# The drain of an attention pipeline from PSUM, and the last expert matmuls in column halves

## The chip, the cores and the metric

The kernel runs on one core of a Trainium2 chip. Its metric is device time in microseconds (us), the median of several runs. A core has TensorE (PE, with its weight loads, PEld), VectorE (DVE), ScalarE (ACT), GpSimd (POOL) and SyncE (SP), which issues the DMAs here. Each runs its own queue in order; semaphores tie them together.

## The reference, cut to what matters

```python
# attention, 4 batches x 8 heads, 576 rows of 64, each row keeps its 32 largest scores
scores = q @ k.T / 8;  kth = 32nd largest of each row
x = softmax(where(scores >= kth, scores, -1e9)) @ v      # as 2304 tokens x 512
# soft mixture of experts, 8 experts with 4 slots each
logits = x @ phi                                          # 2304 x 32
d = exp(logits - logits.max(0));  d /= d.sum(0) + 1e-9
slot_in = (d.T @ x)                                       # 32 x 512
slot_out[e] = relu(slot_in[e] @ w1[e]) @ w2[e]            # w1 512x1024, w2 1024x512
x = softmax(logits, over slots) @ slot_out
# feed-forward, 512 -> 2048 -> 512 with a piecewise quadratic
h = x @ w_in;  g = where(h >= 1, h, where(h <= -1, 0, (h + 1)**2 / 4));  out = g @ w_out
```

## The kernel before, in words

**Attention.** There are 16 pairs (a batch and two heads), each of five row blocks. The step of a block is a token: a letter, the block, for most the head, and behind the point the pair. `S` score matmuls, `C` their copy out of PSUM, `G` and `L` the search for the largest, `M`, `V`, `Y`, `K` the rest of that search (`M` and `Y` on DVE, `V` and `K` on POOL), `P`, `U`, `E` the masked exponential (for the last two blocks of the last pair `U` is a DVE operation, line 853), `T` the transposes, `Q` and `R` their copies, `A` the matmuls with v, `H` the scaled result. A list in the code, `TAIL`, gives the order of the last pairs by hand: each engine takes its own tokens from it in this order.

**The drain.** For the last batch the logits come in three pieces of columns (0 to 256, 256 to 512, 512 to 576; `last_mix`), with tokens `n` + letter + piece: `a`, `b` the logits into PSUM bank n (line 757), `c` their copy to `lT` (760), `d` the running maximum (764, 765), `e` the exponential (773), `f` the factor for the older sum, `t` transposes (782), `g` their copies (791, 794), `w` the weighing of x into `pu` (721), `x` the update of `acc` (798), `l` and `y` bookkeeping on DVE. Block 4 is the middle piece, piece 2. `jp`, `jd` join sums. `fl`, `xc` turn and copy the last x into `xT`. `sp` transposes `acc` (737), `sa` copies it to `siT` (739), which the experts read. All three banks are one tile, `lm_ps`; the transposes `T` of the last pair share one tile of two halves, `lt_ps`, taken in turn.

**The experts.** Two groups of four. `ex_in` multiplies `siT` by w1 (line 1049), `ex_relu`, `ex_turn`, then `ex_out` by w2 (1072) over eight chunks c, four experts side by side in the four column groups; chunks c and c+1 share one loaded tile per expert. `ex_save` copies the result, `ex_place` turns it (1084) and places it in `so128` (1088). `m_first` multiplies by w_in (1129), a copy and a difference follow (1132, 1136), and the first `emit_h` (1207) opens the last stage: 96 steps of one `emit_h` and nine matmuls (1255). `tell`, with a transpose and a maximum, forms a flag that tells if a slower second body must run; `mix_load` to `mix_turn` prepare the combine weights in between.

**The loads.** 88 weight tiles of 512 KB are loaded by SP in one fixed order (`worder`): w1, w2 (with two tiles of w_out in between, as numbers 39 and 40), then w_in and w_out. Each goes to a slot of memory that comes free, and a load waits for its slot's last reader; all behind it on SP wait too. While attention runs there are few slots; `TAIL` frees some with certain tokens (`frees`), as `T31`, `T21`, the last `Y`, `U`, `A`. After attention seven slots `wB0` to `wB6` are laid over the memory of the attention's pools, in the order in which these were opened (`p_work` first, then `p_small`, `p_xT`, `p_xh`, `p_moe`): numbers 39 to 45 of the loads go there, the two w_out tiles first. The next reuse the slots of w1 as `ex_in` ends with them, first those of its chunk 0.

Of the kernel before, what the change touches and what calls it, by code (L numbers as in the profile page):

```python
# [77 lines left out]
Y01.14 m09.11 C30.14 z4.14 O11.14 K10.14 T30.13 Q30.13 S31.14 U31.13 B0.14 L2.14 X10.14 K11.14
E31.13 m10.11 X11.14 C31.14 P00.14 G30.14 Y10.14 U40.13 T31.13 G31.14 M20.14 P01.14 Q31.13 M21.14
Y11.14 A20.13 L3.14 S40.14 R3.13 A21.13 O20.14 U00.14 K20.14 E40.13 C40.14 B1.14 O21.14 T40.13  # L80
Q40.13 X20.14 c0.15 c1.15 S00.15 E00.14 M30.14 K21.14 P10.14 T41.13 G40.14 H2.13 R4.13 U01.14 X21.14
V30.14 c4.15 Y20.14 K30.14 Q41.13 A30.13 P11.14 C00.15 T00.14 E01.14 S01.15 U10.14 Q00.14 M31.14
A31.13 C01.15 E10.14 U11.14 H3.13 Y21.14 T01.14 B2.14 Q01.14 R0.14 V31.14 Y30.14 S10.15 L4.14 X00.15
C10.15 T10.14 S11.15 P20.14 K31.14 Y31.14 E11.14 c5.15 U20.14 Q10.14 C11.15 A40.13 G01.15 P21.14
A41.13 H4.13 M40.14 L0.15 c2.15 B3.14 T11.14 V40.14 lD.13 S20.15 A00.14 U21.14 R1.14 A10.14 P30.14
K40.14 G10.15 E20.14 C20.15 M00.15 Q11.14 Y40.14 P31.14 lN.13 A01.14 T20.14 E21.14 Q20.14 S21.15
H0.14 M01.15 B4.14 A11.14 T21.14 U30.14 C21.15 O01.15 H1.14 S30.15 K01.15 R2.14 Q21.14 G11.15 K00.15
L1.15 E30.14 G20.15 lX.13 X01.15 T30.14 M10.15 U31.14 C30.15 A20.14 c6.15 E31.14 Y00.15 Y01.15
M11.15 B0.15 P40.14 Q30.14 S31.15 lC.13 C31.15 O11.15 U40.14 G21.15 X10.15 K10.15 L2.15 K11.15
T31.14 P01.15 R3.14 P00.15 M20.15 U01.15 A21.14 E40.14 Q31.14 U00.15 M21.15 V20.15 X11.15 S40.15  # L90
H2.14 T40.14 A30.14 E01.15 E00.15 Y10.15 Q40.14 Y11.15 G30.15 B1.15 C40.15 V21.15 A31.14 P10.15
H3.14 T41.14 T00.15 T01.15 U10.15 P11.15 R4.14 Q41.14 A40.14 K20.15 Q00.15 K21.15 A41.14 R0.15
G31.15 Q01.15 E10.15 L3.15 nm3.15 Y20.15 H4.14 P30.15 U11.15 A00.15 Y21.15 B2.15 lD.14 E11.15 A01.15
# [16 lines left out]
def kernel_body(tc, qT, kT, vP, phi, w1, w2, w_in, w_out, out, fast, flag):  # L110
# [633 lines left out]
    def last_mix(k, n):  # L744
# [332 lines left out]
    def ex_save(g):
        h1[g] = p_t.tile([P, 512], F32, name="so_sb", tag="so_sb", bufs=1)
        nc.scalar.copy(h1[g], po_of[g])

    def ex_place(g):
        ps = ps_m.tile([P, 4, P], F32, name="soT_ps", tag="m_ps")
        for c in range(4):
            nc.tensor.transpose(ps[:, c, :], h1[g][:, c * P:(c + 1) * P], ident)
        for e in range(4):
            col = 32 * e + 4 * (4 * g + e)
            s0 = 4 * (4 * g + e)
            nc.vector.tensor_copy(so128[:, :, :, s0:s0 + 4],
                                  ps[:, :, col:col + 4].unsqueeze(2).to_broadcast([P, NHP, 4, 4]))
# [359 lines left out]
```

## Time and profile before

| | us |
|---|---|
| median of 3 runs (772.62 to 773.6) | 773.25 |
| the profiled execution | 771.83 |
| its span, first to last instruction | 770.0 |
| PE busy | 736.8 (96%) |
| DVE, ACT, POOL busy | 651.0, 612.2, 491.7 |
| mean granted TensorE clock | 0.988 |

The profiled execution is one run; its time lies 1.83 us over its span and 1.42 us under the median. In the rows below a stretch is told from the span's start. In a row of a timeline the first number is the start, the second the duration of the merged instructions, and the bracket the idle time of the engine before them and who ended it. PE takes float32 matmuls in two passes, which count as two instructions.

### The profile page before, as it was taken

The numbers are of one execution on the slowest core, as the hardware profiler recorded it, in microseconds if no ns is written. First come the engines' busy times: TensorE is split into PE (matmuls) and PEld (weight loads), VectorE is DVE, ScalarE is ACT, GpSimd is POOL, SyncE is SP. The second block draws the span as 40 slices with busy tenths as digits, with TensorE's granted clock in tenths as the row PEclk, the third lists the DMA queues.
The fourth block names the chain that finished last, engine by engine and source line by source line (L and its number), as shares of the span: only waits on it lengthen the run. The fifth ranks groups of instructions, "written<-read, shape, count | busy, mean of one in ns | idle before, by whom it ended". The sixth has DMA issues, their size and how long they took to land.

```text
span 770.0 us, 15917 instructions
## 1 busy us (share of the span) xinstructions
PE 736.8 (96%) x5014; PEld 542.5 (70%) x5014; DVE 651.0 (85%) x2924; ACT 612.2 (80%) x1300; POOL 491.7 (64%) x532
## 2 busy tenths in 40 slices
PE   4899999999999999999999999898999999999996
PEld 2477777677777677777777788334577788888885
DVE  5999999999999999999999996173899967776662
ACT  4799999999999999999999997243788864554542
POOL 2899999999999999999999995030455400000000
PEclk9899999999999999999999999899999999999998
DMA  7414314304304302202202137999600020100101
GB/s 230 144 59 149 105 47 150 132 25 150 129 22 151 136 19 96 83 15 96 82 20 96 46 105 273 334 406 406 269 0 1 0 83 1 43 10 33 41 1 45
DMA packets 32013, 81.50 MB, mean 106 GB/s; under 512 B 5680, under 2 KB 6576, under 8 KB 31920
## 3 DMA queue, kind: packets, MB, share of 16 engines
q1 hardware_dynamic: 31632, 79.94, 29.1%
q8 instruction: 41, 0.67, 0.4%
q10 hardware_dynamic: 288, 0.46, 0.2%
q14 instruction: 52, 0.43, 0.2%
HBM read 71.25 MB, written 8.91 MB: 104 GB/s over the span
## 4 chain that ended last, share of the span: by engine, by line
PE 58%; DVE 24%; POOL 7%; DMA 6%; issue 2%; ACT 1%; SPq 1%; DVEq 0%; POOLq 0%; ACTq 0%
PE o_ps L1255 19%; PE av_ps L550 10%; PE s_ps L333 6%; PE pt_ps L509 6%; DVE cand L357 5%; DVE top L463 4%; DMA w<-in_moe_w_dram 3%; PE x_ps L333 3%; DVE ghl L1239 3%; POOL ssb L489 3%; DVE cand L362 2%; DVE top L364 2%; POOL mb L416 2%; PE av_ps L548 2%; PE h_ps L1207 2%
## 5 line engine op out<-in xcount | busy, mean ns | idle before, releaser
L1255 PE MATMUL o_ps<-whl,ghl 128*128 128x512 f32 x864 | 216.9, 395 | 1.3 <-DVE ghl L1221 0.5
L1255 PEld LDWEIGHTS o_ps<-whl,ghl 128*128 128x128 f32 x864 | 160.2, 188 | 38.1 <-DVE whl L1201 2.6
L489 POOL TENSOR_TENSOR ssb<-ssb,pen 128x576 f32<-128x576 f32 x141 | 180.3, 1283 | 2.9 <-ACT pen L486 0.4
L357 DVE MAX8 cand<-ssb 128x8 f32<-128x82 f32 (+1 forms) x1008 | 163.7, 235 | 5.4 <-ACT ssb L348 5.4
L550 PE MATMUL av_ps<-v_sb,ptb 128*128 128x65 f32 (+1 forms) x1280 | 143.0, 262 | 0.0
L550 PEld LDWEIGHTS av_ps<-v_sb,ptb 128*128 128x128 f32 (+1 forms) x1280 | 137.1, 181 | 6.3 <-issue 6.2
L1210 ACT ACTIVATE rg<-h_ps,half 128x384 f32<-128x384 f32 (+1 forms) x98 | 56.0, 572 | 68.3 <-PE h_ps L1207 68.3
L333 PE MATMUL s_ps<-kt,qt 64*128 64x288 f32 x512 | 99.5, 466 | 8.7 <-ACT ssb L348 4.4
L416 POOL TENSOR_SCALAR mb<-ssb,top 128x576 bf16<-128x576 f32 x62 | 106.9, 1724 | 0.9 <-DVE top L364 0.9
L348 ACT COPY ssb<-s_ps 128x576 f32<-128x576 f32 x144 | 95.4, 663 | 10.7 <-PE s_ps L333 9.5
L509 PE MATMUL pt_ps<-ident,ssb 128*128 128x128 f32 x600 | 93.8, 279 | 1.9 <-ACT ptb L525 1.8
L509 PEld LDWEIGHTS pt_ps<-ident,ssb 128*128 128x128 f32 x600 | 67.0, 146 | 29.5 <-ACT rs L533 6.8
L1227 DVE SCALAR_TENSOR_TENSOR rg<-h_ps,rg 128x384 f32<-128x384 f32 x95 | 52.7, 555 | 36.4 <-ACT rg L1211 36.3
L492 ACT ACTIVATE ssb<-ssb,kn 128x576 f32<-128x576 f32 x94 | 76.6, 816 | 0.1
L525 ACT COPY ptb<-pt_ps 128x512 f32<-128x512 f32 x120 | 73.0, 608 | 2.3 <-PE pt_ps L509 2.1
L486 ACT ACTIVATE pen<-ssb,kn 128x576 bf16<-128x576 f32 x94 | 73.8, 809 | 1.2 <-POOL kn L482 0.5
L463 DVE MAX8 top<-x_ps 128x8 f32<-128x584 f32 x94 | 71.1, 758 | 3.2 <-PE x_ps L447 2.8
L1190 POOL TENSOR_SCALAR tr_l<-tr_l 128x512 f32<-128x512 f32 x16 | 24.1, 1503 | 77.3 <-DVE tr_l L1189 77.3
L364 DVE MAX8 top<-cand 128x8 f32<-128x56 f32 x432 | 73.0, 206 | 0.1
L1239 DVE TENSOR_TENSOR ghl<-rg,ghl 128x384 fp32r<-128x384 f32 x95 | 67.7, 713 | 5.7
L453 POOL TENSOR_TENSOR w<-ssb,mb 128x576 f32<-128x576 f32 x50 | 64.6, 1293 | 1.2 <-DVE mb L413 1.2
L333 PEld LDWEIGHTS s_ps<-kt,qt 64*128 64x128 f32 x512 | 39.9, 190 | 34.6 <-ACT ssb L348 10.7
(246 smaller groups left out, 1307.2 us busy)
## 6 DMA issues: line engine op xcount, KB each, us to landing
w<-in_moe_w_dram SPq DMA_DIRECT2D x50, 512.0 KB, 6.7
x<-in_moe_w_in_dram SPq DMA_DIRECT2D x16, 512.0 KB, 3.8
w<-in_moe_w_out_dram SPq DMA_DIRECT2D x16, 512.0 KB, 10.3
w<-in_moe_w_dram SPq DMA_DIRECT2D x28, 256.0 KB, 5.7
kt<-in_k_dram SPq DMA_DIRECT2D x15, 360.0 KB, 4.3
v_sb<-in_v_dram SPq DMA_DIRECT2D x16, 325.0 KB, 6.8
qt<-in_q_dram SPq DMA_DIRECT2D x15, 320.0 KB, 5.0
out_dram<-o_sb SPq DMA_DIRECT2D x17, 256.0 KB, 2.3
```

The costliest lines, as they stand in the source:

```text
L333: nc.tensor.matmul(o, q[us], k[us, c:c + o.shape[-1]], start=True, stop=True, tile_position=(j * D, 0), skip_group_check=True)
L348: nc.scalar.copy(ssb[:, 0] if u[1] == NR else ssb[:, :, hf], st.pop((u, hf))[:, :, :HS])
L357: nc.vector.max(st[u]["cand"][:, j, 8 * g:8 * g + 8], row(u, j)[:, S * g // NSEG:S * (g + 1) // NSEG])
L364: nc.vector.max(t8, cand)
L416: nc.gpsimd.tensor_scalar(kept(u, j), row(u, j), t_u, None, op0=ALU.is_ge)
L463: nc.vector.max(st[u]["top"][:, j, TOPU:], src)
L489: nc.gpsimd.tensor_tensor(row(u, j), row(u, j), st.pop((u, "pen", j)), op=ALU.subtract)
L492: nc.scalar.activation(row(u, j), row(u, j), AF.Exp, bias=st[u]["kn"][:, j, 0:1], scale=0.125)
L509: nc.tensor.transpose(pt[:, c, :], pr[:, c0:c0 + P], ident)
L550: nc.tensor.matmul(o, pj[:, c, sl], v_sb[:, 4 * jj + c, :], start=False, stop=(c == NR - 1), skip_group_check=True)
L1239: nc.vector.tensor_tensor(gl, g, gh.bitcast(F32), op=ALU.subtract)
L1255: nc.tensor.matmul(pos[t][n], a[:, sl], w, start=(f == 0 and k == 0), stop=(f == NF - 1 and k == 2))
```

## The change

It replaces `TAIL` by another list. Most tokens are the same; `nx2` is gone, `dg` and four tokens `k` are new. On DVE `M40` now stands ahead of `U31`, and `nd0` ahead of `U40`; on PE `na1` stands ahead of `T30`, and `nb0` ahead of `T21`.

`d` and `e` read the logits from PSUM instead of the copy, which is made later for the bookkeeping. The transposes go to their own columns of the bank. Copies `g` of the first two pieces move from ACT to DVE. Piece 2 no longer weighs into `pu`: `dg` makes a diagonal matrix with the factor of piece 2, `sp` multiplies `acc` by it (a matmul in place of the transpose), and `nw2` adds piece 2, already turned, onto the same PSUM tile with eight small matmuls. `k3`, `k2`, `k4`, `k6` are 3, 2, 4 and 6 bf16 matmuls whose result nobody reads.

The last four chunks of `ex_out` of group 1 run first for columns 0 to 256, then for 256 to 512, each with its own save and place; half of `m_first`'s wide part moves ahead of the second half of its narrow part. `tell` moves from the experts into step 36 of the last stage.

```diff
 TAIL (its last lines)
-U21.15 E21.15 T31.15 T21.15 R3.15 A30.15 Q31.15 nm4.15 V40.15 R2.15 K40.15 P40.15 Q21.15 Y40.15
-U40.15 A31.15 B4.15 A20.15 A21.15 rd3.15 rd2.15 T40.15 B3.15 H3.15 xc1.15 xc0.15 H2.15 T41.15 Q40.15
-Q41.15 R4.15 nb0.15 nc0.15 nd0.15 nl0.15 fl3.15 fl2.15 A40.15 xc2.15 A41.15 rd4.15 na1.15 ne0.15
-xc3.15 H4.15 nb1.15 fl4.15 nt0.15 na2.15 nc1.15 xc4.15 nd1.15 nb2.15 nf0.15 jp.15 ng0.15 nc2.15
-nd2.15 nw0.15 ne1.15 ne2.15 jd.15 ny0.15 nt1.15 nl2.15 nt2.15 nf2.15 nl1.15 ng1.15 nx0.15 nf1.15
-ng2.15 ny1.15 nw1.15 nw2.15 ny2.15 nx1.15 nx2.15 sp.15 sa.15
+rd0.15 G40.15 T11.15 H0.15 V30.15 Q10.15 lX.14 M31.15 R1.15 Q11.15 fl0.15 nm3.15 A10.15 lC.14 K30.15
+Y21.15 P30.15 Y30.15 B2.15 lY.14 xc0.15 V31.15 A11.15 lE.14 U30.15 P20.15 na1.15 P31.15 L4.15 K31.15
+U20.15 P21.15 rd1.15 Y31.15 H1.15 T30.15 U21.15 M40.15 na0.15 Q30.15 E20.15 U31.15 V40.15 E21.15
+fl1.15 T20.15 xc1.15 T31.15 K40.15 Q20.15 nm4.15 Y40.15 nb0.15 R3.15 Q31.15 T21.15 nd0.15 B4.15
+B3.15 A30.15 R2.15 Q21.15 ne0.15 A31.15 P40.15 A20.15 rd3.15 U40.15 H3.15 A21.15 T40.15 rd2.15
+T41.15 H2.15 Q40.15 fl3.15 R4.15 fl2.15 Q41.15 A40.15 xc2.15 xc3.15 A41.15 nb1.15 rd4.15 nt0.15
+H4.15 nd1.15 jp.15 fl4.15 ng0.15 ne1.15 jd.15 na2.15 xc4.15 nf1.15 nc0.15 k3.15 nb2.15 nt1.15 nf0.15
+nd2.15 nw0.15 ng1.15 ne2.15 nl0.15 nw1.15 nf2.15 nx0.15 nc1.15 dg.15 nc2.15 k2.15 nt2.15 nx1.15
+ny0.15 ng2.15 k4.15 sp.15 ny1.15 ny2.15 nw2.15 k6.15 nl1.15 nl2.15 sa.15
...
+        if k == "g":
+            last_ps["g"] = p_work.tile([P, P], F32, name="grown", tag="rs", bufs=3)
+            nc.vector.tensor_scalar(last_ps["g"], ident, sums[len(pieces) - 1]["al"], None, op0=ALU.mult)
+        elif k == "p":
             last_ps["s"] = ps_m.tile([P, P], F32, name="si_ps", tag="m_ps")
-            nc.tensor.transpose(last_ps["s"], acc, ident)
+            nc.tensor.matmul(last_ps["s"], acc, last_ps["g"], start=True, stop=True, skip_group_check=True)
...
-            nc.vector.reduce_max(mb, lT[:, c0:c1], axis=AX.X)
+            nc.vector.reduce_max(mb, lg, axis=AX.X)
...
-            nc.scalar.activation(eT[:, c0:c1], lT[:, c0:c1], AF.Exp, bias=sums[n]["nm"], scale=1.0, accum_out=sb)
+            nc.scalar.activation(eT[:, c0:c1], lg, AF.Exp, bias=sums[n]["nm"], scale=1.0, accum_out=sb)
...
             if mid:
-                for jj in range(2):
-                    sl = slice(jj * REM, (jj + 1) * REM)
-                    nc.scalar.copy(er[sl, jj, :], turned[sl, NR, :])
-            if main:
-                lo, hi = main[0], main[-1] + 1
-                nc.scalar.copy(et[:, lo:hi], turned[:, lo:hi])
+                nc.scalar.copy(e_mid, turned[:, 0, :])
+            else:
+                nc.vector.tensor_copy(et[:, main[0]:main[-1] + 1], turned)
         elif k == "w":
-            weigh(pu, xs, et, main, mid)
+            if mid:
+                si = last_ps["s"]
+                for hp in range(NHP):
+                    for jj in range(2):
+                        sl = slice(jj * REM, (jj + 1) * REM)
+                        nc.tensor.matmul(si[sl, hp * NSLOT:(hp + 1) * NSLOT], xs[hp][0][sl, 8, :], e_mid[sl],
+                                         start=False, stop=True, skip_group_check=True)
+            else:
+                weigh(pu, xs, et, main, False)
...
+        elif name[0] == "k":
+            for _ in range(int(name[1:])):
+                nc.tensor.matmul(last_ps["t"][:, 0, 0], nbig, ident.bitcast(BF16)[:, :P], start=True, stop=True,
+                                 skip_group_check=True)
...
     some(1, 0)
-    tell()
     ex_out(0, range(4))
...
-    ex_out(1, range(4, 8))
-    ex_save(1)
-    ex_place(1)
-    m_first(0, range(NHP))
+    ex_out(1, range(4, 8), 0, 256)
+    ex_save(1, 0, 2)
+    ex_out(1, range(4, 8), 256, 512)
+    ex_save(1, 2, 4)
+    ex_place(1, 0)
+    m_first(0, range(NHP // 2))
+    ex_place(1, 2)
+    m_first(1, range(NHP // 2))
+    m_first(0, range(NHP // 2, NHP))
     m_low(0)
-    m_first(1, range(NHP // 2))
```

## Rows read from the trace of the kernel before

**Rows 1.** Busy time by stretch; last three columns: granted clock, DMA share, GB/s.
```profile
11.50:18.30 6.80, 3.00 (x16) 1.15 (x15) 6.59 (x48) 2.82 (x5) 2.98 (x2) 1.00 0.62 228
...
479.09:485.92 6.83, 5.30 (x44) 3.96 (x44) 2.29 (x13) 3.33 (x16) 0.00 (x0) 1.00 1.04 395
485.92:492.74 6.82, 4.96 (x49) 2.16 (x53) 1.40 (x7) 0.62 (x3) 0.00 (x0) 0.50 0.98 345
```
**Rows 2.** Timeline of the last attention blocks on DVE, PE and ACT.
```profile
469.24 1.06 DVE L853 SCALAR_TENSOR_TENSOR ssb<-ssb,top,ex 128x576 f32<-128x576 f32 x1
470.23 0.80 DVE L413 TENSOR_SCALAR_CACHE_REDUCE mb<-ssb,top 128x576 bf16<-128x576 f32 x1
...
470.45 0.63 PE L509 MATMUL lt_ps<-ident,ssb 128*128 128x128 f32 x4 [0.46 <-DVE ssb L853]
...
471.72 0.59 ACT L525 COPY ptb<-lt_ps 128x512 f32<-128x512 f32 x1 [0.23 <-PE lt_ps L509]
...
478.38 0.69 PE L550 MATMUL av_ps<-v_sb,ptb 128*64 128x65 f32 x10
```
**Rows 3.** Timeline of the drain, in order of the engines' starts.
```profile
478.99 1.99 PE L757 MATMUL lm_ps<-xT,phi_sb 128*128 128x256 f32 x8
...
481.58 0.88 PE L757 MATMUL lm_ps<-xT,phi_sb 128*128 128x64 f32 x6
482.50 0.37 ACT L760 COPY lT<-lm_ps 128x256 f32<-128x256 f32 x1 [2.62 <-PE lm_ps L757]
...
482.91 0.42 DVE L764 TENSOR_REDUCE mb<-lT 128x1 f32<-128x256 f32 x1 [3.43 <-ACT lT L760]
...
483.51 0.21 ACT L794 COPY et<-lm_ps 128x64 f32<-128x64 f32 x1 [0.33 <-PE lm_ps L757]
...
483.73 0.52 ACT L773 ACTIVATE eT<-lT,nmn 128x256 f32<-128x256 f32 x1
...
483.89 0.64 PE L721 MATMUL lm_ps<-xh,et 128*32 128x128 f32 x16 [0.25 <-ACT lT L760]
...
485.36 0.21 ACT L794 COPY et<-lm_ps 128x64 f32<-128x64 f32 x1 [0.35 <-PE lm_ps L285]
...
485.60 0.35 DVE L798 SCALAR_TENSOR_TENSOR acc<-acc,al,lm_ps 128x128 f32<-128x128 f32 x1 [0.56 <-ACT et L794]
...
485.99 0.37 ACT L791 COPY er<-lm_ps 64x32 f32<-64x32 f32 x2 [0.22 <-DVE acc L798]
```
**Rows 4.** Timeline of the first expert matmuls.
```profile
489.73 11.97 PE L1049 MATMUL h<-w,siT 128*32 128x512 f32 x96 [0.35 <-ACT siT L739]
```
**Rows 5.** SP's waits, 478 to 500 us: total, times, longest.
```profile
SPq L196 <- PE lm_ps L721: 3.6, 1, 3.6
SPq L196 <- PE rq_ps L728: 2.3, 1, 2.3
```
**Rows 6.** SP's timeline: the loads numbers 39 and 40.
```profile
480.46 0.86 SPq L196 DMA_DIRECT2D w<-in_moe_w_out_dram  x2
```
**Rows 7.** DMA issues with us to landing: at 471.22, 480.46, 493.60 and 518.69 us.
```profile
w<-in_moe_w_dram SPq DMA_DIRECT2D x1, 512.0 KB, 3.6
...
w<-in_moe_w_out_dram SPq DMA_DIRECT2D x1, 512.0 KB, 6.6
...
w<-in_moe_w_dram SPq DMA_DIRECT2D x1, 512.0 KB, 7.0
...
w<-in_moe_w_dram SPq DMA_DIRECT2D x1, 256.0 KB, 6.6
```
**Rows 8.** Timeline of the experts' end and the start of the last stage.
```profile
524.04 3.64 PE L1072 MATMUL so<-w,h1T 128*32 128x512 f32 x32
...
527.83 0.58 ACT L1079 COPY so_sb<-so 128x512 f32<-128x512 f32 x1 [3.18 <-PE so L1072]
...
529.84 2.45 PE L1129 MATMUL m_ps<-w,so 128*128 128x128 f32 x12 [0.71 <-DVE so L1088]
...
532.47 1.45 PE L1129 MATMUL m_ps<-w,so 128*128 128x384 f32 x4
```

More of the change, by code (lines that the diff above doesn't have):

```diff
@@ L77 @@
 TAIL = '''
[L78 to L93, printed above, removed]
@@ L100 @@
-xc3.15 H4.15 nb1.15 fl4.15 nt0.15 na2.15 nc1.15 xc4.15 nd1.15 nb2.15 nf0.15 jp.15 ng0.15 nc2.15
-nd2.15 nw0.15 ne1.15 ne2.15 jd.15 ny0.15 nt1.15 nl2.15 nt2.15 nf2.15 nl1.15 ng1.15 nx0.15 nf1.15
-ng2.15 ny1.15 nw1.15 nw2.15 ny2.15 nx1.15 nx2.15 sp.15 sa.15
+m09.11 z4.14 U31.13 C30.14 T30.13 Y01.14 O11.14 S31.14 K10.14 Q30.13 B0.14 L2.14 X10.14 K11.14
+C31.14 U40.13 E31.13 X11.14 m10.11 P01.14 M20.14 S40.14 c0.15 E40.13 Y10.14 T31.13 P00.14 G30.14
+A20.13 M21.14 Q31.13 O20.14 G31.14 T40.13 R3.13 A21.13 Q40.13 U00.14 Y11.14 C40.14 T41.13 O21.14
@@ new lines @@
+L3.14 B1.14 c1.15 K20.14 S00.15 K21.14 U01.14 H2.13 X20.14 M30.14 C00.15 R4.13 E00.14 S01.15 c4.15
+V30.14 M31.14 X21.14 Q41.13 P10.14 G40.14 A40.13 V31.14 P11.14 A41.13 C01.15 Y20.14 T00.14 E01.14
+U10.14 A30.13 Y21.14 Q00.14 L4.14 H4.13 K30.14 A31.13 E10.14 B2.14 U11.14 P20.14 T01.14 H3.13 S10.15
+Y30.14 Q01.14 K31.14 c5.15 X00.15 C10.15 G01.15 P21.14 S11.15 U20.14 Y31.14 R0.14 T10.14 E11.14
+L0.15 A00.14 Q10.14 B3.14 U21.14 E20.14 T11.14 lD.13 C11.15 A01.14 M00.15 lN.13 Q11.14 c2.15 M40.14
+S20.15 R1.14 M01.15 H0.14 T20.14 E21.14 G10.15 A10.14 C20.15 K00.15 Q20.14 G11.15 V40.14 A11.14
@@ new lines @@
+O01.15 P30.14 L1.15 S21.15 K01.15 K40.14 T21.14 H1.14 C21.15 U30.14 lX.13 P31.14 Y40.14 X01.15 R2.14
+M10.15 Q21.14 U31.14 S30.15 E30.14 Y00.15 A20.14 lC.13 B4.14 K10.15 M11.15 P40.14 G20.15 lY.13
+C30.15 A21.14 Y01.15 E31.14 c6.15 T30.14 G21.15 O11.15 S31.15 H2.14 Q30.14 B0.15 X10.15 L2.15 K11.15
+C31.15 U40.14 T31.14 lE.13 P00.15 X11.15 M20.15 R3.14 P01.15 U00.15 S40.15 Y10.15 E40.14 U01.15
+Y11.15 Q31.14 A30.14 C40.15 G30.15 E00.15 T40.14 B1.15 V20.15 A31.14 M21.15 Q40.14 E01.15 T41.14
+G31.15 K20.15 H3.14 P11.15 V21.15 T00.15 Y20.15 R4.14 P10.15 T01.15 K21.15 L3.15 Q41.14 A40.14
@@ new lines @@
+U10.15 R0.15 Q00.15 A41.14 Q01.15 A00.15 H4.14 U11.15 M30.15 E10.15 A01.15 lD.14 lN.14 E11.15 T10.15
+rd0.15 G40.15 T11.15 H0.15 V30.15 Q10.15 lX.14 M31.15 R1.15 Q11.15 fl0.15 nm3.15 A10.15 lC.14 K30.15
+Y21.15 P30.15 Y30.15 B2.15 lY.14 xc0.15 V31.15 A11.15 lE.14 U30.15 P20.15 na1.15 P31.15 L4.15 K31.15
+U20.15 P21.15 rd1.15 Y31.15 H1.15 T30.15 U21.15 M40.15 na0.15 Q30.15 E20.15 U31.15 V40.15 E21.15
+fl1.15 T20.15 xc1.15 T31.15 K40.15 Q20.15 nm4.15 Y40.15 nb0.15 R3.15 Q31.15 T21.15 nd0.15 B4.15
@@ L752, in last_mix @@
         lg = bank[:, :c1 - c0]
-        turned = bank[:, :(NR + 1) * NSLOT].rearrange("p (r s) -> p r s", s=NSLOT)
+        turned = bank[:, 3 * P:3 * P + 2 * NSLOT].rearrange("p (r s) -> p r s", s=NSLOT)
         pu = bank[:, 2 * P:3 * P]
@@ L1065, in ex_turn, with ex_out @@
             nc.vector.tensor_copy(hT[:, 4 * n:4 * n + 4, :], ps)
-    def ex_out(g, cs):
+    def ex_out(g, cs, lo=0, hi=512):
         if g not in po_of:
@@ L1071, in ex_out, with ex_save, ex_place @@
             for e in range(4):
-                nc.tensor.matmul(po_of[g][32 * e:32 * e + 32, :], h1T[g][:, c, 32 * e:32 * e + 32],
-                                 wtile[(1, 4 * g + e, c // 2)][c % 2],
+                nc.tensor.matmul(po_of[g][32 * e:32 * e + 32, lo:hi], h1T[g][:, c, 32 * e:32 * e + 32],
+                                 wtile[(1, 4 * g + e, c // 2)][c % 2][:, lo:hi],
                                  start=(c == 0), stop=(c == 7), tile_position=(0, 32 * e),
                                  skip_group_check=True)
[L1077 to L1089, printed above, removed]
+    def ex_save(g, lo=0, hi=NHP):
+        if lo == 0:
+            h1[g] = p_t.tile([P, 512], F32, name="so_sb", tag="so_sb", bufs=1)
+        nc.scalar.copy(h1[g][:, lo * P:hi * P], po_of[g][:, lo * P:hi * P])
+    def ex_place(g, lo):
+        ps = ps_m.tile([P, 3, P], F32, name="soT_ps", tag="m_ps")
+        for c in range(2):
+            nc.tensor.transpose(ps[:, c, :], h1[g][:, (lo + c) * P:(lo + c + 1) * P], ident)
+        for c in range(2):
+            mine = ps.rearrange("p c s -> p (c s)")[:, c * P + 16 * g:c * P + 16 * g + 144]
+            mine = mine.rearrange("p (e s) -> p e s", s=36)[:, :, :4]
+            nc.vector.tensor_copy(so128[:, lo + c, :, 16 * g:16 * g + 16].rearrange("p r (e s) -> p r e s", s=4),
+                                  mine.unsqueeze(1).to_broadcast([P, 4, 4, 4]))
     def tell():
@@ L1122, in m_first @@
         lo, hi = ((0, P), (P, 512))[part]
-        if not part:
+        if not part and cs[0] == 0:
             mx[part] = ps_m.tile([P, P], F32, name="m_ps0", tag="m_ps")
-        elif cs[0] == 0:
+        elif part and cs[0] == 0:
             mx[part] = ps_f.tile([P, 512], F32, name="m_ps3", tag="e_ps")[:, :hi - lo]
@@ L1287, in step @@
             mhl.extend(m_split())
+        if i == 36:
+            tell()
         if i % 4 == 0 and i >= 40:
@@ L1352, in kernel_body @@
     ex_out(1, range(2))
-    ex_place(0)
+    ex_place(0, 0)
+    ex_place(0, 2)
     mix_turn(2)
```

14 lines of the change are left out of this document (5 added, 9 removed).

## The prediction

> **What bounds the kernel now.** I read the busy shares by stretch first, then the timeline between 465 and 535 us, SP's waits, and the landing of single loads. TensorE has work nearly throughout; the change touches the one place where it does not, the drain and the experts, 479 to 533 us. There three things run. First a chain of small steps through PSUM: from the end of `A41` (478.38 + 0.69 = 479.07) to the first expert matmul (489.73) it takes 10.66 us [rows 2, 4]. Second the clock: in 485.92 to 492.74 half of 2.4 GHz is granted, after a stretch in which PE was busy for 5.30 of 6.83 us with mostly narrow work [rows 1]; 3.0 us of the expert matmuls fall into it, which costs them 1.5 us [rows 1, 4]. Third, and this decides, the weights: the DMA share is about 1 [rows 1], a load of 512 KB at 395 to 410 GB/s takes 1.28 us, and the last part of w2, issued at 518.69, lands 6.6 us later at 525.3 [rows 7]. PE reads that tile in the third chunk of the block that starts at 524.04; a chunk takes 3.64/4 = 0.91 us, so at 525.9 or a little later [rows 8]. The weights are only 0.6 us ahead. A drain that ends early is worth nothing beyond that unless the stream of loads moves too.
>
> **How the steps of the drain are ordered.** The reader should look at the brackets of [rows 3]. The copy of piece 1 (482.50) could run once its logits were there, at 478.99 + 1.99 = 480.98; ACT idled 2.62 us until the matmuls of piece 2, in another bank, had ended (481.58 + 0.88 = 482.46). The copy at 483.51 waits for piece 2's logits, the weighing of piece 0 (483.89) for a copy out of piece 2's bank, the copy at 485.36 for piece 2's transposes, the update of `acc` with piece 0 (485.60) for a copy of piece 1, the next copy (485.99) for that update, though both only read. Six such waits say: all accesses to the tile `lm_ps` by different engines go one after another in the order of `TAIL`. `lt_ps` behaves alike: the copy at 471.72 of the half that `T31` had filled by 471.08 started after `T21` [rows 2].
>
> A rule of the Trainium skill speaks for less order: PSUM — Partial Sum Buffer, section PSUM bank collisions raise a hardware error, says that two engines must be kept apart on one bank and quadrant, while different banks run clean together. The rows above show waits across banks, so the trace does not agree that this is all; what it would give is a rival below.
>
> **The change, part by part.**
>
> *Order of the last blocks.* On DVE `M40` (0.80) now precedes `U31`, which ended at 470.30 [rows 2]. With DVE full there, `T31` starts 0.8 later. In the new list `Q20` and `Q31` stand between `T31` and `T21`; one behind another on `lt_ps` they hold `T21` for two copies of 0.59 and the copy `R3`, some 1.35 more than before, of which `nb0` (two passes of 256 columns, a quarter of 1.99, 0.5) fills a part that it used after `T41`. On the other side stand pauses of DVE ahead of this, which I put at up to 1.5. Sum for the end of `A41`: 0.8 + 1.35 - 0.5 - 0.75 (half the pauses) = 0.9 later, 480.0; bounds -0.5 and +1.7.
>
> *The chain.* After `A41` the new list is `nb1 nt0 nd1 ng0 ne1 na2 nc0 nb2 nt1 nd2 nw0 ng1 ne2 nw1 nx0 nc1 nc2 nt2 nx1 ng2`, and nearly each changes the engine. With the durations of [rows 3] and 0.03 to 0.05 per change: `nb1` 0.5, `nt0` 0.2, `nd1` 0.45 + 0.2, `ng0` 0.2 (as ACT's 0.21), `ne1` 0.55, `na2` 0.9, `nc0` 0.4, `nb2` 0.45, `nt1` 0.2: 4.05. Then `nd2` 0.25 (0.42 for a quarter of the columns, with its start-up), `nw0` 0.7, `ng1` 0.25, `ne2` 0.4, `nw1` 0.65, `nx0` 0.4, `nc1` and `nc2` 0.65, `nt2` 0.45: 3.75, so 7.8. `nx1` 0.4, `sp` 0.4: 8.6 after `A41`. `ng2` runs beside `sp`, `nw2` 0.5 (16 passes of 32 columns; 0.64 for 16 of 128 is its upper bound, 0.25 the lower), `sa` 0.3: 9.4. Before it was 10.66. So the skipped copies, the second update and the weighing in place bring 1.2, not the 3 and more that one gets by counting them one by one; the reads of the logits by DVE and ACT from PSUM are three new links of the same chain. First expert matmul: 480.0 + 9.4 = 489.4, 0.3 earlier.
>
> *The small matmuls* lie in pauses of PE and cost nothing if they end before the next link; 15 of them at under 0.1 are 1.5 at most, of which a tail of 0.2 could show. Whether they keep the clock up I leave open: PE still pauses for each link, and at worst 6.8 us at half clock in the expert matmuls cost 3.4 instead of 1.5, at best nothing. The next step hides either.
>
> *The loads.* `grown` takes a buffer of `p_work`, the first pool of the attention. `wB0` and `wB1` lie over it, so load number 39 waits for `sp`, its reader. That these loads wait for single readers is seen in [rows 5]: SP waits 2.3 us for the end of the logits and 3.6 us for the weighing. Number 39 was issued at 480.46 and landed at 487.1 [rows 6, 7]. Now it goes at 480.0 + 8.6 = 488.6 and lands, with an empty queue as at 471.22, 3.6 us later [rows 7]: 492.2, 5.1 late. SP is in order, so the 49 loads behind it come after. Part is won back: before, the eighth load behind number 39 landed at 493.60 + 7.0 = 500.6, 13.5 us after it, where eight loads take 10.3; the 3.3 lost were waits for the last weighing and for the first expert chunk, and in the new order these readers are done when SP comes there. Net 5.1 - 3.3 = 1.8 late: the last part of w2 lands at 527.1. Bounds: 4.0 us of latency instead of 3.6 (+0.4); `A41` at its bounds (-1.4, +0.8).
>
> *The halves.* PE reaches the third chunk at about 522.5 to 524.5, by the clock, and stands until 527.1. Then it still has one expert's two passes (0.45 for 256 columns), a chunk (0.45) and the second half of four chunks (1.82), with 0.1 to start: 529.9, against 524.04 + 3.64 = 527.7. That is 2.2 late; the halves bring the need for the last tile forward by 0.9 and leave as much work behind it as before.
>
> *Behind them* the first half is saved by then, so copy, turn and place (527.83 to 529.84, 2.0) shrink to turn and place of half the columns, about 1.0; but half of the wide `m_first` (1.45 for four passes) now stands ahead of the second half of the narrow one, and the second half's turn stands between, together some 0.7 not paid before [rows 8]. Net -0.3, between -1.0 and +0.4.
>
> *The flag.* `tell` leaves a place that PE now spends waiting (0 gained) and adds a small transpose to a full stage, at most its part of 0.63 for four [rows 2]: +0.15.
>
> **Sum**: 2.2 - 0.3 + 0.15 = +2.05; I take +1.9, for pauses not seen. The profiled execution's 771.83 becomes 773.7. The median shown is 1.42 higher, 773.25, and becomes 775.1.
>
> **Rivals.**
>
> *The order holds per bank only* (the skill's rule). Then `nb2` need not wait for `nc0`, nor `nw0` for `nd2`, nor `nw1` for `ne2`; `sp` ends some 5.8 after `A41`, at 485.8, number 39 lands at 489.4, 2.3 late, less 3.3: w2 is complete at 524.3, PE at 527.1, 0.55 early. With -0.3 and +0.15: -0.7, 772.5. Against it: the six waits.
>
> *`grown` holds no load back*, because its buffer lies elsewhere. Then the stream recovers some 2.5 at the first expert chunk, w2 no longer binds, and the 0.3 of the chain, a part of the clock's 1.5 and the -0.3 come through: -1.2, 772.0; with both rivals together some -2.7, 770.5, which is the faster side. Decided by the issue time of number 39: under 486.6 the change gains, above it loses. For: only that the trace of before has no such reader.
>
> *The clock falls during the wait for w2.* Half was granted after stretches with PE busy for 5.30 of 6.83 us, and for 3.00 of 6.80 [rows 1]; a wait of 3 us or more makes such a stretch. The second half, the narrow and wide `m_first` and the first step, 1.8 + 2.0 + 0.7 us of PE work, would take up to twice as long: +2 to +4, so 778. Against it: if the clock falls in the drain again, PE comes later and the wait is short.
>
> *The drain's order costs nothing* and `A41` ends where it did: 0.9 less on all that follows, 774.2.
>
> **How the numbers follow.** A difference under 0.2% (1.55 us) cannot be told from none here. Forecast 0.55 (its own range 773.9 to 776.6; two thirds of it above the bound), order per bank 0.12, `grown` without effect 0.10 and both together 0.05, the clock 0.10, the order for nothing 0.08. Faster: both together, a third of the `grown` case, a little of the per-bank case, and pauses that I count wrongly: 0.17. Slower: 0.36 + 0.10 and some: 0.47. Within: 0.36. The range leaves out half of the clock's case and the both-together case: 771.4 to 777.4.
>
> **What would show it.** SP's first w_out load after attention at 487.5 to 489 instead of 480.46, with DMA share well under 1 ahead of it; PE waiting on a DMA in `ex_out` of group 1; first expert matmul at 489 to 490; waits between `lm_ps` accesses of different banks. Wrong: that load before 486.6, or no DMA wait at w2's end.

## The result and the profile after

The changed kernel takes 780.92 us in the median of 6 runs (779.93 to 781.76), the kernel before, run beside it, 773.02 (772.48 to 773.66): 1.0 % slower, ratio between 1.0089 and 1.011. The forecast was +1.9 us, the measurement is +7.9. The profiled execution has a span of 780.0 instead of 770.0. These 10.0 are 2.1 more than the medians show, because of which execution was profiled: the one of before took 771.83, 1.2 under its median, the one of after 781.76, 0.8 over its median and the slowest of the six. Of the 10.0, 0.5 are there from the start: the same score matmuls stand 0.5 later at 300 us already.

**The last attention blocks**, DVE and PE of the timeline after:

```profile
471.72 0.81 DVE L862 SCALAR_TENSOR_TENSOR ssb<-ssb,top,ex 128x576 f32<-128x576 f32 x1
472.23 1.09 PE L509 MATMUL lt_ps<-ident,ssb 128*128 128x128 f32 x8 [0.52 <-ACT ssb L492]
474.71 0.66 PE L509 MATMUL lt_ps<-ident,ssb 128*128 128x128 f32 x4 [0.85 <-ACT ptb L525]
481.57 0.69 PE L550 MATMUL av_ps<-v_sb,ptb 128*64 128x65 f32 x10
```

`U31` ends at 472.53 (before 470.30), `T21` starts at 474.71, behind two copies out of `lt_ps`, and `A41`, the last row here, ends at 482.26 instead of 479.07 [rows 2]: 3.2 later, 2.7 without the 0.5 of the start.

**The drain**, from the same timeline, the links in which the order or the clock shows:

```profile
484.00 0.47 ACT L778 ACTIVATE eT<-lm_ps,nmn 128x256 f32<-128x256 f32 x1 [0.94 <-DVE run_s L730]
484.62 1.34 PE L762 MATMUL lm_ps<-xT,phi_sb 128*128 128x64 f32 x6 [0.76 <-ACT eT L778]
486.00 0.37 ACT L765 COPY lT<-lm_ps 128x256 f32<-128x256 f32 x1 [1.14 <-PE lm_ps L762]
486.42 0.69 PE L762 MATMUL lm_ps<-xT,phi_sb 128*128 128x64 f32 x2
487.85 1.08 PE L721 MATMUL lm_ps<-xh,et 128*32 128x128 f32 x16 [0.39 <-DVE mb L769]
489.71 1.08 PE L721 MATMUL lm_ps<-xh,et 128*32 128x128 f32 x16 [0.78 <-ACT eT L778]
492.98 0.80 PE L742 MATMUL si_ps<-grown,acc 128*128 128x128 f32 x2
493.71 1.07 PE L802 MATMUL si_ps<-e_mid,xh 64*64 64x32 f32 x16
494.71 0.82 PE L912 MATMUL lt_ps<-ident,nbig 128*128 128x128 bf16 x6
495.68 1.08 PE L1062 MATMUL h<-w,siT 128*32 128x512 f32 x4
```

The brackets show the forecast order: `na2` waits for `ne1` of another bank, `nw0` for `nd2`, `nw1` for `ne2`. New are the durations. The first weighing took 0.64 before [rows 3] and takes 1.08. From the end of `A41` to the end of `sp` it is 11.5 us (492.98 + 0.80 - 482.26), forecast 8.6. The busy shares by stretch say why (columns as in rows 1):

```profile
479.00:484.87 5.87, 5.11 (x48) 3.98 (x48) 1.43 (x8) 2.85 (x12) 0.00 (x0) 1.00 0.96 334
484.87:491.70 6.83, 4.94 (x47) 3.25 (x46) 1.44 (x6) 1.52 (x7) 0.00 (x0) 0.50 0.35 122
491.70:498.53 6.83, 6.51 (x47) 3.67 (x51) 1.63 (x8) 0.57 (x4) 0.00 (x0) 0.50 0.55 184
498.53:505.36 6.83, 6.83 (x68) 2.14 (x64) 0.00 (x0) 1.03 (x2) 0.00 (x0) 1.00 1.02 410
```

TensorE is granted half of 2.4 GHz from 484.87 to 498.53, 13.7 us instead of the 6.8 of before [rows 1], and most of it now lies in the chain. DMA share and GB/s are low in the same stretches, because the loads have stopped (SP's wait, next).

**The loads**: SP's waits, its timeline, and single issues with us to landing (at 493.81, at 499.46 and the last of w2 at 527.88):

```profile
SPq L196 <- PE si_ps L742: 10.2, 1, 10.2
```
```profile
493.81 0.80 SPq L196 DMA_DIRECT2D w<-in_moe_w_out_dram  x2
494.71 5.13 SPq L196 DMA_DIRECT2D w<-in_moe_w_dram  x7
```
```profile
w<-in_moe_w_out_dram SPq DMA_DIRECT2D x1, 512.0 KB, 3.6
...
w<-in_moe_w_dram SPq DMA_DIRECT2D x1, 512.0 KB, 10.3
...
w<-in_moe_w_dram SPq DMA_DIRECT2D x1, 256.0 KB, 6.4
```

SP waits 10.2 us for `sp`, the reader of `grown`. Number 39 goes at 493.81 (before 480.46) and lands at 497.4, the eighth behind it at 509.8, the last part of w2 at 534.3 instead of 525.3 [rows 6, 7]: 9.0 late.

**The experts' end**, timeline of PE and ACT:

```profile
529.68 2.02 PE L1085 MATMUL so<-w,h1T 128*32 128x256 f32 x20
533.02 1.94 PE L1085 MATMUL so<-w,h1T 128*32 128x256 f32 x12 [1.31 <-DMA w<-in_moe_w_dram]
535.05 0.37 ACT L1093 COPY so_sb<-so 128x256 f32<-128x256 f32 x1 [4.76 <-PE so L1085]
535.47 1.93 PE L1085 MATMUL so<-w,h1T 128*32 128x256 f32 x32 [0.52 <-ACT so_sb L1093]
```

PE stands for the loads: the first column half takes 5.3 us (529.68 to 534.96), the second, whose tiles are there by then, 1.9. The second also waits 0.52 for the copy of the first, though it writes other columns. PE ends w2 at 537.4 instead of 527.7 [rows 8]. The first output leaves 88.8 us behind that (626.21), before 89.1 (616.75). From there to the end it is 153.8 us, before 153.3.

### The profile page after: what moved, and what is told of

Same layout as the page of the kernel before. It is cut to its first block, busy times and chain, and to the rows that moved or that the text cites. A ratio compares the mean times of both kernels' runs of the same rounds, so it can differ in the third digit from the quotient of the medians.

```text
span 780.0 us, 16008 instructions
## 1 busy us (share of the span) xinstructions
PE 745.7 (96%) x5047; PEld 548.4 (70%) x5062; DVE 651.9 (84%) x2926; ACT 611.8 (78%) x1298; POOL 491.0 (63%) x532
## 4 chain that ended last, share of the span: by engine, by line
PE 56%; DVE 22%; POOL 8%; ACT 7%; DMA 4%; issue 3%; ACTq 0%; DVEq 0%; POOLq 0%; SPq 0%
PE o_ps L1269 18%; PE av_ps L550 9%; PE s_ps L333 6%; PE pt_ps L509 5%; DVE cand L357 4%; DVE top L463 4%; DVE ghl L1253 3%; DMA w<-in_moe_w_dram 3%; POOL ssb L489 3%; PE x_ps L333 3%; POOL mb L416 2%; DVE cand L362 2%; PE h_ps L1221 2%; DVE top L364 2%; PE h L1062 2%
## 5 line engine op out<-in xcount | busy, mean ns | idle before, releaser
L333 PE MATMUL s_ps<-kt,qt 64*128 64x288 f32 x512 | 101.2, 473 | 9.1 <-ACT ssb L348 4.9
L333 PEld LDWEIGHTS s_ps<-kt,qt 64*128 64x128 f32 x512 | 40.3, 192 | 36.4 <-ACT ssb L348 13.5
## 6 DMA issues: line engine op xcount, KB each, us to landing
w<-in_moe_w_out_dram SPq DMA_DIRECT2D x16, 512.0 KB, 10.2
```

The lines of the kernel that those rows point to most:

```text
L333: nc.tensor.matmul(o, q[us], k[us, c:c + o.shape[-1]], start=True, stop=True, tile_position=(j * D, 0), skip_group_check=True)
```

## The experiments

"Theory A" and "rival" are those of the expectation printed with each run; "won" is against the kernel that it was made from. The chain is counted from the end of `A41` to the end of the first pass of `sp`, the experts from the first `ex_in` matmul to the end of `ex_out`; the half clock is the stretch with 0.50 granted between 478 and 500 us. All three are from one profile each, the medians from 4 to 12 runs; the kernel before had 773.02 to 773.21 in the five sets.

| | us | chain | experts | half clock |
|---|---|---|---|---|
| before | 773.0 | 10.3 | 38.0 | 6.8 |
| changed | 780.92 | 11.3 | 41.7 | 13.7 |
| 1 grown apart | 778.21 | 10.1 | 38.9 | 10.2 |
| 2 old blocks | 780.95 | 14.0 | 41.9 | 13.7 |
| 3 ends only | 773.80 | 10.6 | 39.2 | 10.2 |
| 4 hold only | 775.90 | 9.9 | 41.0 | 6.8 |
| 5 = 1 + fillers | 775.13 | 9.2 | 37.8 | 0 |
| 6 = 1 - small | 777.97 | 11.2 | 38.9 | 13.7 |
| 7 = 1 + own tile | 774.29 | 7.1 | 38.8 | 3.4 |
| 8 chain alone | 777.87 | 14.0 | 37.3 | 13.7 |
| 9 before + fillers | 770.69 | 9.5 | 36.5 | 0 |
| 10 = 7 + fillers | 773.27 | 7.0 | 39.7 | 0 |
| 11 both old | 770.29 | 8.3 | 36.5 | 0 |
| 12 = 11 - fillers | 772.81 | 8.1 | 39.0 | 6.8 |
| 13 changed + fillers | 779.51 | 9.2 | 41.6 | 0 |
| 14 = 11 + halves | 771.51 | 8.3 | 39.0 | 0 |
| 15 = 10 + old end | 772.06 | 7.0 | 37.1 | 0 |

**1. `grown` apart.**

```diff
-            last_ps["g"] = p_work.tile([P, P], F32, name="grown", tag="rs", bufs=3)
+            last_ps["g"] = phi_sb[:, 0].rearrange("p g s -> p (g s)")
```

> The changed kernel with `grown` in another memory, over which no load lies. Theory A (held loads: number 39 waits for the reader of `grown`, issued 493.8 and landed 497.4, and all w2 with it): number 39 goes soon after A41, at 483 to 485, five loads are ahead, the last part of w2 lands at 528 to 531 instead of 534.3 and PE no longer waits for it; the experts then end 37 to 38 us after their first matmul at 495.7, at 533.5 instead of 537.4: 777.0 us against 780.9. Theory B (the late A41 and the long chain cost it all, the loads would be late anyway): within 0.7 of 780.9, with DMA waits left at the end of w2.

778.21 (ratio to before 1.0042 to 1.0083), 2.7 won. SP's timeline:

```profile
483.95 1.94 SPq L196 DMA_DIRECT2D w<-in_moe_w_out_dram  x2
486.77 8.41 SPq L196 DMA_DIRECT2D w<-in_moe_w_dram  x5
```

Number 39 goes at 483.95 and the last of w2 lands at 529.7; PE no longer waits for a load and ends w2 at 533.6, as theory A had it. The median gives 2.7 where 3.9 were expected. `grown` holds the loads, but by itself it is a third of the loss.

**2. The old order of the blocks.** `TAIL` up to `H4.15` as before, without `nc0` and `nl0`, then the new drain.

> The changed kernel with the old order of all tokens up to H4 of the last pair; the drain behind it, its PSUM chain and `grown` stay. Theory A: A41 ends about 2.7 earlier (479.6), the first matmuls of piece 1 stand behind it again and cost 0.7; the loads held by `grown`, and with them everything, move by 2.0: 778.9 us. Rival (the order of the blocks is hidden, the chain starts when it starts for another reason): 780.9 within 0.5.

780.95: no gain, as the rival had it. `A41` ends 3.6 earlier, at 478.6, and the chain is 2.6 longer:

```profile
480.14 0.47 ACT L777 ACTIVATE eT<-lm_ps,nmn 128x256 f32<-128x256 f32 x1 [2.36 <-PE lm_ps L761]
...
480.91 0.70 PE L761 MATMUL lm_ps<-xT,phi_sb 128*128 128x256 f32 x2 [0.81 <-ACT xT L630]
```

`ne0`, which now reads piece 0 in PSUM, waits for the matmuls of piece 1 that stand ahead of it in the list; the copy `xc3` stands behind `ne0` on ACT, and `nb1` waits for `xc3`. So `nb1` (480.91) starts 2.3 behind the end of `A41`, in the changed kernel (482.18) 0.1 ahead of it: that is most of the 2.6. Reading from PSUM put the operation into the order of the tile, and that ate most of what the blocks gave. The clock fell earlier too, at 482.7; what that cost is not told apart here.

**3. The experts' end alone.** The kernel before with `ex_out`, `ex_save`, `ex_place`, `m_first` in halves and `tell` in step 36.

> The kernel before with the column halves at the experts' end and the moved flag alone. Theory A: w2's last tile lands as before (525.3), the second half waits 0.5 for the copy of the first, behind the halves 0.3 are won: 773.4 us, between 772.8 and 774.0. Rival (the halves are a main part of the loss: loads of narrower matmuls and two more turns): 774.5 to 776.

773.80, ratio 0.9997 to 1.0018: 0.6 above the kernel before, which the interval doesn't tell from none, and not a main part of the loss. Its half clock was 10.2 us long, by chance of the execution as it seems, since up to there its instructions are those of before.

**4. The hold alone.** The kernel before, with

```diff
+            last_ps["g"] = p_work.tile([P, P], F32, name="grown", tag="rs", bufs=3)
+            nc.vector.tensor_copy(last_ps["g"], ident)
-            nc.tensor.transpose(last_ps["s"], acc, ident)
+            nc.tensor.transpose(last_ps["s"], acc, last_ps["g"])
```

> The kernel before, and `sp` transposes with a copy of the identity that lies where `grown` lies in the changed kernel; DVE makes the copy between nd2 and nw0, all else is as before. Theory A: load number 39 goes when `sp` has ended, at 489.4 instead of 480.5, lands at 493.0 instead of 487.1; of the 5.9 between 1.3 (as the changed kernel showed) and 3.3 (as I forecast) are won back, w2 is 2.6 to 4.6 late: 776 to 778 us. Rival (the stream recovers before w2 binds): 773.0 to 773.6.

775.90 (1.0027 to 1.0049): +2.7, just under the 776 to 778 expected and the same as experiment 1 took away. SP's waits and timeline:

```profile
SPq L195 <- PE si_ps L739: 8.6, 1, 8.6
```
```profile
490.26 0.81 SPq L195 DMA_DIRECT2D w<-in_moe_w_out_dram  x2
```

Counted from the end of `A41`, number 39 goes 8.6 later than before and lands 5.5 later; w2's last part lands 3.8 later. So 1.7 are won back here, and PE waits 0.7 for a load at the end.

**5. Fillers.** Kernel 1; the small matmuls get 256 columns and stand as `k6` behind `fl4`, `k3` `na2`, `k2` `nt1`, `k4` `nw0`, `k6` `nw1`, `k4` `nt2`, `k3` `nw2`.

```diff
-                nc.tensor.matmul(last_ps["t"][:, 0, 0], nbig, ident.bitcast(BF16)[:, :P], start=True, stop=True,
+                nc.tensor.matmul(last_ps["t"][:, 0, :2].rearrange("p a b -> p (a b)"), nbig, ident.bitcast(BF16), start=True, stop=True,
```

> The changed kernel with `grown` out of the loads' way (the first experiment, 778.2 us) and the small matmuls doubled in columns (256) and spread over seven pauses (28 in place of 15). Theory A (the chain is 2.9 longer than I forecast since its matmuls ran at half clock, 0.50 granted from 484.9 to 498.5): if these keep the clock at 1.00 up to the experts, the chain from A41 to the end of `sp` takes 8.5 to 9.2 instead of 10.05, and 1.4 to 2.8 come back in the experts: 775.5 to 776.5 us. If the clock falls nevertheless, the fillers take twice as long and delay links: 778 to 779.5. Rival (the chain's length is the semaphores and small instructions, not the clock): the clock stays up and the chain still takes 10 or more.

775.13 (1.0011 to 1.0031), 3.1 won, a little more than expected. The clock stayed at 1.00 from 26 to 770 us and the chain took 9.2.

**6. Without the small matmuls.** Kernel 1 without the four `k` tokens.

> The first experiment's kernel (778.2 us) without any of the 15 small matmuls. Theory A: they don't keep the clock up; the first expert matmul no longer waits for the last six (0.5 to 0.6 behind the copy to siT), the half clock begins at the same place or one step earlier: 777.4 to 778.2. Rival (they hold the clock for a while): the half clock begins 3 us or more earlier, the chain grows by over 1 and the time is 779 or more.

777.97: the time is that of theory A, 0.2 from kernel 1. Two signs of the rival are there as well: against kernel 1, the half clock began at 484.95 instead of 488.22, and the chain took 11.2 instead of 10.1. But in the changed kernel, with the 15 in place, it began at 484.87, so one execution each doesn't show whether they hold it off for a while; they did not keep the drain at 1.00 in either kernel, and leaving them out costs nothing in the median. One thing is won: the first expert matmul follows the copy to `siT` within 0.05 instead of 0.59.

**7. A tile of its own for piece 2.** Kernel 1 with

```diff
-        bank = last_ps["b"][:, n]
+        if mid and "m" not in last_ps:
+            last_ps["m"] = ps_s.tile([P, 512], F32, name="lm_mid", tag="pt_ps", bufs=1)
+        bank = last_ps["m"] if mid else last_ps["b"][:, n]
```

and `xc4` ahead of `ne1`.

> The first experiment's kernel (778.2 us) with piece 2 in a PSUM tile of its own (and the copy xc4 ahead of ne1 on ACT). Theory A (all accesses to one tile go in the list's order, across its banks): nb2 no longer waits for nc0, nw0 not for nd2, nw1 not for ne2; the chain from A41 to the end of `sp` shrinks from 10.05 to 8.3 to 9.2, the time to 776.7 to 777.5. Rival (the order on each engine alone makes the chain): the chain is as long within 0.3, 778.2.

774.29 (1.0003 to 1.0028), 3.9 won, more than expected. The chain is 3.0 shorter. PE's timeline:

```profile
485.85 0.39 PE L763 MATMUL lm_mid<-xT,phi_sb 128*128 128x64 f32 x2
486.16 0.31 PE L788 MATMUL lm_ps<-ident,eT 32*128 32x32 f32 x2
486.40 0.65 PE L720 MATMUL lm_ps<-xh,et 128*32 128x128 f32 x16
```

`nb2`, `nt1` and `nw0` follow one another without a wait. Piece 2 had a bank of its own before as well, so the order is one of the tile: with two tiles these waits across the pieces are gone. The clock also stayed up to 491.52, in kernel 1 to 488.22, which the expectation had not counted, so the 3.9 are not the order's alone, and `xc4` was not moved by itself. The comparison at a clock of 1.00 on both sides is 5 with 10: there the chain is 2.2 shorter and the time 1.9.

**8. The chain alone.** Old blocks and old experts' end, the chain from PSUM, `grown` apart.

> The kernel before with the new chain alone: old order of the tokens up to H4, `grown` out of the loads' way, old experts' end. Theory A: against before the chain is no shorter, since its links change the engine and its matmuls fall under the half clock (in the second experiment A41 to the end of `sp` took 13.96 against 10.3 before); without the hold of the loads 773 to 775.5 us. Rival (the chain itself is a gain and only `grown` and the order of the blocks spoil it): 771 to 772.5.

777.87 (1.0039 to 1.0075), worse than either theory: with one tile and the old list the chain takes 14.0, of which 9.9 under the half clock (483.70 to 493.57), and costs 4.8 with it.

**9. The kernel before and fillers.** `k3` behind `na2`, `k1` behind `nb2`, `k6` behind `nt2` and `nw2`, `k1` behind `sp`, nothing else.

> The kernel before, and in five pauses of its drain 17 bf16 matmuls of 256 columns whose result nobody reads. Theory A (in the drain the clock falls for the quiet of PE, and that alone costs 1.5 in the first expert matmuls and 0.7 in the last weighing): it stays at 1.00, the experts begin 0.5 to 0.7 earlier and their first group runs 1.5 faster; as the last tile of w2 is only 0.6 ahead of PE, no more than 0.5 to 1.2 of it comes out at the end: 772.0 to 772.6 us. Rival (w2's last tile decides alone and doesn't move): 773.0 within 0.3, with a wait of PE for that tile.

770.69 (0.996 to 0.998): 2.5 faster than before, twice the most that was expected. The stretch that was granted 0.57 in the kernel before:

```profile
485.00:492.00 7.00, 6.07 (x77) 3.09 (x81) 2.17 (x10) 1.49 (x8) 0.00 (x0) 1.00 0.98 373
```

The experts take 36.5 instead of 38.0, the chain 9.5 instead of 10.3, and PE never waits for w2: its last part lands at 523.0 (before 525.3). SP, which waited 5.0 us for the slots that `ex_in` frees, waits 3.9.

**10. Own tile and fillers.** Kernel 7 with 19 matmuls of 256 columns (`k3` behind `fl4`, `k2` `na2`, `k3` `nw0`, `k7` `nw1`, `k2` `nt2`, `k2` `nw2`).

> The seventh experiment's kernel (`grown` out of the way, piece 2 in its own tile, 774.29 us) with 19 matmuls of 256 columns in six pauses in place of the 15 of 128. Theory A: the half clock, there 3.4 us long from 491.5, is gone, which gives 1.2 to 1.6 in the first expert matmuls; the loads let a part through: 773.0 to 773.8. Rival (the loads, held by the last weighing that reads xh, decide by now): 774.3 within 0.3 and a wait of PE at the end of w2.

773.27 (0.9991 to 1.0009), as theory A, though PE waits 1.2 for w2, which was a sign of the rival.

**11. Put together.** Old blocks with `ne0` and `xc3` ahead of `na1`, own tile, the 19 fillers, `grown` apart, old end.

> The chain from PSUM put together from what the runs showed: `grown` out of the way, piece 2 in its own tile, the 19 fillers, the old order of the blocks with ne0 and xc3 ahead of the first matmuls of piece 1, and the old experts' end. Theory A: A41 ends as before (479.1), `sp` ends at 487.4 to 488.2 instead of 489.4, the experts start at 488.7 to 489.3 with the clock at 1.00; then w2's last tile limits the gain to 1.0 to 2.0: 771.0 to 772.2 us. Rival (w2 moves with the last weighing, which is no earlier than before): 773.0 within 0.4.

770.29 (0.9951 to 0.9977), better than expected and the fastest, 2.9 under the kernel before and 10.6 under the changed one. Chain 8.3, clock at 1.00. Against kernel 9, which has none of the chain from PSUM, it is 0.4 faster, less than the spread of the runs (769.57 to 770.77 and 769.82 to 773.57).

**12. The same without small matmuls.**

> The kernel of the experiment before this one (both old orders, own tile) without any of the small matmuls. Theory A: the clock falls to 0.50 for 3.4 to 10 us and takes 1 to 2.5 back: 772.3 to 774. Rival (the clock costs nothing once the loads decide): the same time as with fillers within 0.3.

772.81 (0.9982 to 1.0001): the fillers are worth 2.5 here too. The clock fell at 487.92 for 6.8 us.

**13. The changed kernel with the fillers of 5 alone.**

> The changed kernel with nothing else than the 28 fillers of 256 columns of the fifth experiment in place of its 15 small matmuls; `grown` still holds the loads. Theory A (of the 2.9 by which its chain was longer than forecast, the half clock made 2.0 or more): A41 to the end of `sp` 9.1 to 9.4 instead of 11.3, load number 39 issued 2.0 earlier behind A41, w2 2.0 earlier: 778.5 to 779.3 us instead of 780.9; what the clock gives back in the experts is lost to the wait for w2. Rival (the chain is long by its order alone): 780.9 within 0.4.

779.51 (1.0065 to 1.0098), 1.4 won, a little less than expected; the chain takes 9.2 as expected and w2 lands at 531.4 instead of 534.3. Two stretches:

```profile
478.00:485.00 7.00, 7.00 (x65) 5.61 (x65) 2.14 (x9) 3.34 (x14) 0.00 (x0) 1.00 1.00 350
485.00:492.00 7.00, 6.25 (x76) 4.07 (x77) 2.47 (x11) 1.85 (x9) 0.00 (x0) 1.00 0.31 111
```

The clock stays up, the DMA share still falls to 0.31: with the loads held, more than half of the 3.1 that the fillers give in 5 is lost again to the wait for w2 (the experts take 41.6).

**14. The best kernel with the halves.** Kernel 11 with the new experts' end and flag.

> The best kernel so far (both old orders, own tile, fillers, 770.29 us) with the column halves and the moved flag added. Theory A (the second half waits 0.5 for the copy of the first, and the last tile is needed 0.9 earlier): slower by 0.3 to 0.8, 770.6 to 771.1. Rival (the halves were only covered by the wait for w2 and now win 0.3 or more): 769.5 to 770.0.

771.51 (0.9963 to 0.9985), 1.2 slower than kernel 11, somewhat more than theory A said. PE's waits from 488 to 545 us, the largest two:

```profile
PE h_ps L1222 <- DVE m L1151: 1.2, 2, 0.7
PE so L1086 <- DMA w<-in_moe_w_dram: 1.2, 1, 1.2
```

Kernel 11 has no wait for w2. The last part of w2, with us to landing, here (issued at 516.87) and in kernel 11 (at 516.76):

```profile
w<-in_moe_w_dram SPq DMA_DIRECT2D x1, 256.0 KB, 7.7
...
w<-in_moe_w_dram SPq DMA_DIRECT2D x1, 256.0 KB, 6.5
```

In 6.5 us it would have been there at 523.4, when PE came to it (524.66 - 1.22). So the 1.2 in this profile is the late landing of one execution. What comes from the order is the 0.5 for the copy; what the earlier need for the last tile costs shows in 15.

**15. Kernel 10 with the old end.**

> The tenth experiment's kernel (new order of the blocks, own tile, fillers, 773.27 us) with the old experts' end; against the best so far it differs by the order up to H4 alone. Theory A (A41 late by 2.7 costs its part now that the chain is short): 772.2 to 772.9, 2.0 or more above 770.29. Rival (the order of the blocks is free, as in the second experiment, and the column halves made the difference): 770.3 to 771.2.

772.06 (0.9982 to 1.0001), 1.8 above kernel 11, a little less than expected: that is the new order of the blocks, once the chain no longer hides it. Against kernel 10 the old end wins 1.2, as in 14; here the earlier need shows: in kernel 10 the last part of w2 lands at 526.31 and PE ends w2 3.1 behind it (529.42), here it lands at 526.73 and PE ends 1.3 behind it (528.04).

## Why the prediction was wrong

The direction and the place were right: `grown` holds number 39 until `sp`, the order is one of the tile, PE waits for w2, the halves win nothing. The size was not. From the changed kernel's profile, number 39 goes 13.4 later than before where 8.1 were forecast, and 1.3 of it are won back where 3.3 were forecast; these two make w2 9.0 late instead of 1.8. Of the 7.2 that are missing, the chain is 2.9 (11.5 for 8.6), the loads that were to win time back 2.0, the end of `A41` 1.8 (2.7 for 0.9) and the start of this execution 0.5.

- **The small matmuls and the clock: the step that failed.** I costed the small matmuls at 0, left the clock open, priced it only in the expert matmuls (1.5 to 3.4), and wrote that the next step hides either. But the chain's own matmuls run at that clock too, and the chain sets when the loads go. It took 11.5 instead of 8.6; with the clock at 1.00 it takes 2.1 less (13 against the changed kernel; first pass 11.3 to 9.2). That is the largest single part of the 5.3 by which number 39 went later than forecast; the other 0.8 of the chain stay at full clock and are not traced further. In medians, mending the clock alone gives 1.4 (13) and mending the hold alone 2.7 (1). The Trainium skill, TensorE: Matmul & The Clock Gate, section Part 1: The HAM clock gate, says that the throttled state is the default and that activity releases it. The runs agree: with fillers of 256 columns 1.00 is granted throughout the drain in 5, 9, 10, 11, 13, 14 and 15, and the ten other profiles, among them 6 and 12 without any small matmuls, all show 3.4 to 13.7 us at 0.50.
- **The end of `A41`** was forecast 0.9 late and was 2.7 late. `M40` ahead of `U31` and the two copies ahead of `T21` are there as forecast; the half of DVE's pauses (0.75) that I set against them did not come. In the last 10 us up to the end of `U31` DVE paused 0.86, in one piece ahead of 463.99, where it had paused 0.48. `U31` ended 1.7 late without the 0.5 of the start: 0.8 is `M40`, 0.4 the longer pause, the rest is not traced. What undoing costs or gives depends on the rest: 0 in experiment 2, 1.8 between 15 and 11.
- **The loads**: the landing after 3.6 was right. The 3.3 to win back were not there: the eighth load landed 12.4 behind number 39, before 13.5, where I had written 10.3. The queue was empty, and on its refill the third load landed 3.4 us after the second (498.67, 502.09); only then one came per 1.28. The 2.1 that this gap has over 1.28 are the difference between 10.3 and 12.4.
- **The halves**: PE ended w2 3.1 behind the last landing, forecast 2.8; the wait of the second half for the copy of the first (0.52) I did not see, though the rule of one order for a tile, which I had read out of the drain, says it. That the halves leave as much work behind the last tile as before was wrong: with the old end PE ends 1.3 behind it (15). In the median the new end costs 1.2, in 14 against 11 and in 10 against 15.
- **Behind them** -0.3 + 0.15 was forecast; from the end of w2 to the first output it is 88.8 against 89.1, -0.3. From the first output to the end it is 0.5 more; the kernels here spread by 0.8 in that stretch, so this says nothing of the flag.

Of the rivals, the order per bank falls with the brackets of the drain above (`na2` waits for `ne1` of another bank) and with 7 (the waits go with the tile), and that `grown` holds nothing falls with 1 and 4. The clock did not fall in the wait for w2 (1.00 from 498.5 on) but earlier, and that was worse. That `A41` ends where it did falls with the 2.7; that undoing its delay gains nothing holds only in the changed kernel (2).

The steps from the changed kernel to the best, in this order: `grown` -2.7, fillers -3.1, own tile -1.9, old end -1.2, old blocks -1.8, together the 10.6. Another order splits them otherwise (the own tile ahead of the fillers gives 3.9, the fillers with the loads held 1.4), so no step has a price of its own. The 10.6 are more than the 7.9 that were lost because fillers speed up the kernel before as well (2.5, experiment 9).

Open stays how much of this holds in the median execution: only one of each kernel was profiled, and the half clock began at different places in kernels with the same instructions up to there (485.17 in experiment 3, 485.92 before).

## What to carry to other kernels

In a drain of short, dependent matmuls the granted clock can be part of the chain: here it fell to half, and the chain took 11.3 us instead of 9.2. Look at it there first, and try fillers in the pauses before the chain is rebuilt. A new buffer in a pool whose memory is overlaid later makes its reader a gate for all loads that stand behind in the queue, so place it where nothing is laid over. Splitting work over parts of one tile gave no overlap here, since the order was kept per tile: what is to run side by side needs tiles of its own.

## Not expected of the hardware

Seventeen matmuls whose result nobody reads make the tuned kernel 2.5 us faster (9). The clock fell though PE was busy 5.11 of the 5.87 us before (changed kernel). The half clock lasted 3.4, 6.8, 10.2 or 13.7 us in different kernels, and 10.2 in experiment 3 against 6.8 before, with the same instructions up to its start.
